# Loading the output rows of one head in eleven small transfers during the attention loop instead of one transfer after the last values

## The chip, the cores and the metric

The kernel runs on one core of a Trainium2 chip. The metric is the device time of one execution in microseconds (us). The figure for the kernel before is the median of 7 runs, 194.99 us, with the runs between 194.86 and 195.08 us. A profile of one execution (its own time is 194.87 us) gives the start and length of every instruction, the packets of the DMA engines, and the time at which each DMA engine reported its part of a transfer as landed.

## What is computed

One decode step: a single token `x` of 512 numbers is normalised; an attention branch of 32 heads reads the last 4096 keys and values of a long cache; a small MLP branch makes a gate; the two are joined.

```python
xn = _layernorm(x)
# attention branch, W = 4096, 32 heads of 128
q = (xn @ wq).reshape(B, Sq, Hq, Dh).transpose(0, 2, 1, 3)
k = k_cache[:, :, Sk - W:, :]
v = v_cache[:, :, Sk - W:, :]
p = softmax(einsum("bhqd,bhkd->bhqk", q, k) * Dh ** -0.5)
o = einsum("bhqk,bhkd->bhqd", p, v)
s = o.transpose(0, 2, 1, 3).reshape(B, Sq, Hq * Dh) @ wo
# gate: an MLP of xn
out = x + s * silu(B(xn))
```

Keys and values are bf16. For 32 heads they are 32 MB and 32 MB, `wq` and `wo` are 4 MB each, and the MLP's weights about 3 MB, so nearly 79 MB are read once and little is done with each byte.

## The kernel before, in words

The 32 heads are worked through in `NG = 8` groups of `G = 4`. A group's keys are one tile `kv` of 128 partitions x 128 columns x 128 numbers (4 MB), and so are its values. The loop at L513 runs `s` from 0 to 9. Step `s` loads and scores the keys of group `s`; the values belong to group `h = s - LAG`, two steps behind. Keys have three buffers (`K_BUFS`), values two (`V_BUFS`).

All large loads are issued by one queue, SyncE's (SP), in the order in which the program names them (`load`, L78). An SP load waits, on the queue, until the buffer that it will fill has been read for the last time and until its semaphore is free: there are eight semaphores for DMAs, used in turn, so a load also waits for the landing of the load eight places before it. The order of the instructions on TensorE (PE), VectorE (DVE) and ScalarE (ACT) is the program's own inside the loop (`manual_schedule`, L509).

The loads before the loop are the MLP's weights `w2`, `w3`, `w4`, two loads of 20 rows each into `w4_few` (L97), and `wq` (L101). The loop's loads on SP are then: keys 0 (in two halves), 1 and 2; values 0; keys 3, values 1; keys 4, values 2; keys 5, values 3, and the rows of `wo` for heads 0 to 15; keys 6, values 4; keys 7, values 5, and the rows of `wo` for heads 16 to 23 and 24 to 27; values 6; values 7. Values 7 come in four pieces of 64, 32, 16 and 16 columns (`cuts`, L508). Behind them come the rows of `wo` for heads 28 to 31, 128 rows of 512 numbers (1 KB) for each head, into the tile `wo_rows` [128 partitions, 4 heads, 512]: heads 28 and 29 in one DMA, 30 in one, 31 in one (L524). This is the last load before the output.

The end of the program (L595 to L609): PE multiplies the pieces of values 7 with the probabilities as they land (`v_part`, L440: 64, then 32 + 16, then 16 matmuls), DVE divides the result (`v_out`, L457), PE adds the four heads' output to the sum `y_ps` with `y_head` (L505; four matmuls for each head against `wo_row(h)`, recorded at L156 because `rows_add` makes them), DVE applies the gate (L606) and adds `x` (L608), and SP stores 1 KB (L609). `y_block(2)` a little earlier does the same kind and number of matmuls (16, L156) for heads 24 to 27.

The memory of `wo_rows` and of the value buffers is taken at step `s = LAG` (L517 to L521), from the place where the weights (`wts`) stood until then.

Of the kernel before, what the change touches and what calls it, by code (L numbers as in the profile page):

```python
# [8 lines left out]
P = 128  # L9
# [9 lines left out]
G = 4  # L19
LAG = 2  # L20
# [9 lines left out]
def kernel(  # L30
# [18 lines left out]
    _, H, Sk, Dh = A_k_cache.shape  # L49
# [28 lines left out]
    def load(dst, src):  # L78
        return tc.keep_in_program_order(nc.sync.dma_start(out=dst, in_=src))
# [23 lines left out]
    def load_kv(pool, cache, g, cuts=(0, CP)):  # L103
        t = pool.tile([P, CP, Dh], BF16, tag="kv", name="kv")
        src = cache[0, G * g:G * g + G, W0:, :].rearrange("a (b c) d -> b a (c d)", b=PB)
        dst = t[:].rearrange("p c d -> p (c d)")
        for c0, c1 in zip(cuts, cuts[1:]):
            load(dst[:, c0 * Dh:c1 * Dh], src[:, :, c0 * Dh:c1 * Dh])
        return t
# [43 lines left out]
    def rows_add(ps, col, w, last):  # L153
        k = col.shape[0]
        for j in range(KC):
            nc.tensor.matmul(ps[32 * j:32 * j + 1, :], lhsT=col, rhs=w[0:k, j * P:(j + 1) * P],  # L156
                             start=False, stop=last, skip_group_check=True)
# [161 lines left out]
    def k_open(g):  # L319
        st[g] = {  # L320
            "sT": ps_s.tile([P, CP - 64, G], FP32, tag="sT", name="sT"),
            "S": sm_pool.tile([P, CP], FP32, tag="S", name="S"),
        }

    def k_vector(g, kn, part):
        m = nd(g) // 4
        rows = slice(m * part, m * part + m)
        prod = prod_pool.tile([P, 20, Dh], BF16, tag="prod", name="prod")
        nc.vector.tensor_tensor(out=prod[:, 0:m, :], in0=kn[:, rows, :],  # L329
                                in1=q_bc[:, g:g + 1, :].to_broadcast([P, m, Dh]), op=ALU.mult)  # L330
        nc.vector.tensor_reduce(out=st[g]["S"][:, rows], in_=prod[:, 0:m, :], axis=AX.X, op=ALU.add)  # L331
# [3 lines left out]
    def batches(g):  # L335
        n, m = nd(g), CP - nd(g)
        k = -(-m // 8)
        edges = [n + m * i // k for i in range(k + 1)]
        return list(zip(edges, edges[1:]))

    def k_turn(g, kn, b):
        c0, c1 = batches(g)[b]
        pt = ps_tr.tile([P, 8, P], BF16, tag="pt", name="pt")
        for c in range(c0, c1):
            nc.tensor.transpose(pt[:, c - c0, :], kn[:, c, :], ident_bf[:])  # L345
        kts[b] = kt_pool.tile([P, 8, P], BF16, tag="kt", name="kt")
        nc.scalar.copy(out=kts[b][:, 0:c1 - c0, :], in_=pt[:, 0:c1 - c0, :])  # L347

    def k_scores(g, b):
        kt = kts.pop(b)  # L350
        c0, c1 = batches(g)[b]
        for c in range(c0, c1):
            nc.tensor.matmul(st[g]["sT"][:, c - nd(g), :], lhsT=kt[:, c - c0, :],  # L353
                             rhs=qT_bf[:, G * g:G * g + G], start=True, stop=True)


    def sm_own(g):
        s = st[g]
        m = CP - nd(g)
        s["own"] = sm_pool.tile([P, CP - 64, G], FP32, tag="own", bufs=1, name="own")  # L360
        for a in range(G):
            nc.scalar.mul(s["own"][:, 0:m, a], s["sT"][:, 0:m, a], par[:, a:a + 1])  # L362
# [31 lines left out]
    def sm_den(g):  # L394
        s = st[g]
        s["den"] = ps_misc.tile([P, G], FP32, tag="misc", name="den_ps")
        nc.tensor.matmul(s["den"][:], lhsT=ones_f[:], rhs=s["sum"][:], start=True, stop=True)

    def sm_rden(g):
        s = st[g]  # L400
        s["rden"] = sm_pool.tile([P, G], FP32, tag="rden", name="rden")
        nc.vector.reciprocal(out=s["rden"][:], in_=s["den"][:])  # L402
# [7 lines left out]
    def load_wo(i):  # L410
        h0, n = blocks[i]
        load(wo_blk[i], A_wo[h0 * P:(h0 + n) * P, :].rearrange("(p t) n -> p t n", p=P))
# [4 lines left out]
    def load_rows(h, n):  # L417
        load(wo_rows[:, h - h_part:h - h_part + n, :],
             A_wo[h * P:(h + n) * P, :].rearrange("(h p) n -> p h n", p=P))
# [23 lines left out]
    def v_add(g):  # L443
        s = st[g]
        s["oT"] = ps_misc.tile([P, G], FP32, tag="misc", name="oT")
        for j in range(4):
            nc.tensor.matmul(s["oT"][:], lhsT=s["ov_sb"][:, j, :], rhs=fold[:, G * j:G * j + G],  # L447
                             start=(j == 0), stop=(j == 3))

    def v_out(g):  # L450
        h = G * g
        b = [i for i, (h0, _) in enumerate(blocks) if h >= h0][-1]
        if b not in o_blk:
            o_blk[b] = sm_pool.tile([P, blocks[b][1]], BF16, tag=f"o{b}", bufs=1, name="o")
        c = h - blocks[b][0]
        if g >= NG - 3:
            nc.vector.tensor_tensor(out=o_blk[b][:, c:c + G], in0=st[g]["oT"][:], in1=st[g]["rden"][:],  # L457
                                    op=ALU.mult)
            return
        for k in range(G):  # L460
            nc.scalar.mul(o_blk[b][:, c + k:c + k + 1], st[g]["oT"][:, k:k + 1], st[g]["rden"][:, k:k + 1])  # L461
# [48 lines left out]
                                         mybir.EngineType.Activation})  # L510
    region.__enter__()
    v_pool = None
    for s in range(NG + LAG):  # L513
        h = s - LAG
        last = h == NG - 1
        kn = load_kv(k_pool, A_k_cache, s, (0, 64, CP) if s == 0 else (0, CP)) if s < NG else None
        if s == LAG:  # L517
            wts_guard.__exit__(None, None, None)
            v_pool = ctx.enter_context(tc.tile_pool(name="v", bufs=V_BUFS))
            wo_blk[2] = v_pool.tile([P, 4, D], BF16, tag="wo_4", bufs=1, name="wo_4")  # L520
            wo_rows = v_pool.tile([P, H - h_part, D], BF16, tag="wo_rows", bufs=1, name="wo_rows")  # L521
        if last:
            v = load_kv(v_pool, A_v_cache, h, cuts)
            for r, n in ((H - G, 2), (H - 2, 1), (H - 1, 1)):  # L524
                load_rows(r, n)
        elif h >= 0:
            v = load_kv(v_pool, A_v_cache, h)
        if h == 3:
            wo_24 = k_pool.tile([P, 32, D], BF16, tag="kv", name="wo_24")
            wo_blk[0], wo_blk[1] = wo_24[:, 0:16, :], wo_24[:, 16:24, :]  # L530
            load_wo(0)
        if h == 5:
            load_wo(1)
            load_wo(2)

        if s < NG:
            nb = len(batches(s))

            def keys(b0, b1):
                for b in range(b0, b1):  # L540
                    k_turn(s, kn, b)
                    if b > 0:
                        k_scores(s, b - 1)

            k_open(s)
            k_vector(s, kn, 0)
            keys(0, 2)
            if s > 1:
                sm_den(s - 2)
                sm_rden(s - 2)  # L550
            if h - 1 in MOVED:
                v_add(h - 1)
                v_out(h - 1)
            if s == 7:
                rows_add(y_ps, one_f, y_row, False)
            keys(2, 4)
            k_vector(s, kn, 1)
            if s > 0:
                sm_turn(s - 1)
            if s == 6:  # L560
                ox_spread(0)
            keys(4, nb)
            k_scores(s, nb - 1)
            sm_own(s)
            if s > 0:
                sm_exp(s - 1)
            k_vector(s, kn, 2)
            if s == 6:
                ox_pick(0)
            k_vector(s, kn, 3)  # L570
            if h >= 0:
                v_part(h, v)
            sm_max(s)
            if s == 6:
                y_wide(0, 0, 16)
            if h >= 0 and h not in MOVED:
                v_out(h)
        elif s == NG:

            sm_den(NG - 2)  # L580
            sm_rden(NG - 2)
            sm_turn(NG - 1)
            sm_exp(NG - 1)
            v_add(h - 1)
            v_out(h - 1)
            ox_spread(1)
            ox_pick(1)
            sm_den(NG - 1)
            sm_rden(NG - 1)
            y_block(1)  # L590
            v_part(h, v)
            v_add(h)
            v_out(h)
            ox_spread(2)
        else:  # L595
            v_part(h, v, 0, cuts[1])
            ox_pick(2)
            y_block(2)
            for c0, c1 in zip(cuts[1:], cuts[2:]):
                v_part(h, v, c0, c1)  # L600
            v_out(h)
            for r in range(H - G, H):
                y_head(r)
# [36 lines left out]
```

## Time and profile before

| | |
|---|---|
| median of 7 runs | 194.99 us (194.86 to 195.08) |
| the profiled execution | 194.87 us, its span 193.1 us |
| PE busy | 138.2 us, 72% of the span |
| DVE busy | 145.6 us, 75% |
| ACT busy | 90.7 us, 47% |
| bytes read from HBM | 78.84 MB, 408 GB/s over the span |
| share of the 16 DMA engines taken by SP's queue (q1) | 96.0% |
| last SP load of values 7 issued | 173.63 us from the start of the span |
| three `wo_rows` loads issued | 174.28 us and the two after it |
| output store issued | 190.35 us |

The span is the time that the profile covers; the 1.8 us that are missing to the execution's own time lie around it. The page gives a share of busy time for each engine and a row for the DMA engines. A share is an average; which wait ends last at a place is read from the chain of waits and from the timeline. "16 DMA engines" are sixteen movers that share each transfer: every one moves its part, and a transfer has landed when all that take part have reported.

### The profile page before, as it was taken

The page shows a single profiled execution, that of the slowest core. Times are in us where ns is not written, and L with a number is a line of the kernel's source. Part 1 is how long each engine was busy: PE and PEld are TensorE (multiplying, and loading weights), DVE is VectorE, ACT ScalarE, POOL GpSimd, SP SyncE. Part 2 cuts the span into 40 slices and gives each one's busy share as a digit, 9 for nine tenths or more (in the row PEclk, how much of TensorE's full clock was granted, in tenths as well). Part 3 has the DMA queues.
Part 4 walks back from the last instruction along what each step waited for, and adds up shares of the span by engine and source line. Part 5 has one row for each costly group of instructions (what it writes and reads, how often), then busy time and mean ns, then how long its engine had stood idle before and what let it go on. Part 6 is the DMA issues. An engine that isn't in the chain of part 4 may idle for free.

```text
span 193.1 us, 3919 instructions
## 1 busy us (share of the span) xinstructions
PE 138.2 (72%) x1696; PEld 99.9 (52%) x1696; DVE 145.6 (75%) x168; ACT 90.7 (47%) x197; POOL 5.9 (3%) x12
## 2 busy tenths in 40 slices
PE   0548978989965169429787892875497989877882
PEld 0437248868854153328547632851395348636371
DVE  1580021999999999998999999999999988962011
ACT  2002001888778354407873753474358245863100
POOL 8210000000000000000000000000000000000000
PEclk9999985555555555855876558587655596695755
DMA  6999999999999999999999998999999999999980
GB/s 211 414 434 434 424 434 441 426 434 431 434 431 436 434 424 434 434 434 434 431 428 434 424 428 384 455 428 434 438 421 428 433 428 389 452 431 411 403 315 5
DMA packets 4722, 79.08 MB, mean 410 GB/s; under 512 B 666, under 2 KB 1210, under 8 KB 1722
## 3 DMA queue, kind: packets, MB, share of 16 engines
q1 hardware_dynamic: 4554, 78.84, 96.0%
q8 instruction: 13, 0.21, 0.5%
q10 hardware_dynamic: 152, 0.00, 0.0%
q14 instruction: 3, 0.02, 0.0%
HBM read 78.84 MB, written 0.00 MB: 408 GB/s over the span
## 4 chain that ended last, share of the span: by engine, by line
DVE 50%; PE 29%; DMA 9%; ACT 4%; issue 4%; SPq 1%; POOL 0%; POOLq 0%; ACTq 0%
DVE S L331 29%; DVE prod L329 15%; DMA kv<-in_A_v_cache_dram 7%; PE pt L345 6%; PE oT L447 4%; ACT kt L347 3%; PE hr_ps L255 3%; PE ov L431 3%; PE a_ps L236 2%; PE sT L353 2%; DMA x_bf<-in_A_x_dram 2%; PE yr_ps L495 2%; PE qT_ps L271 2%; PE hr_ps L250 1%; DVE S L367 1%
## 5 line engine op out<-in xcount | busy, mean ns | idle before, releaser
L331 DVE TENSOR_REDUCE S<-prod 128x20 f32<-128x2560 bf16 (+2 forms) x32 | 82.2, 2570 | 1.1
L347 ACT COPY kt<-pt 128x1024 bf16<-128x1024 bf16 (+1 forms) x56 | 55.2, 1005 | 16.7 <-PE pt L345 15.7
L345 PE MATMUL pt<-ident_bf,kv 128*128 128x128 bf16 x444 | 51.4, 293 | 2.3 <-DMA kv<-in_A_k_cache_dram 2.3
L345 PEld LDWEIGHTS <-kv 128*128 128x128 bf16 x444 | 41.9, 136 | 7.2 <-issue 3.5
L329 DVE TENSOR_TENSOR prod<-kv,q_bc 128x2560 bf16<-128x2560 bf16 (+2 forms) x32 | 43.5, 1359 | 1.6 <-ACT q_bc L285 1.3
L353 PE MATMUL sT<-qT_bf,kt 128*128 128x4 bf16 x444 | 20.9, 169 | 13.2 <-ACT kt L347 12.2
L353 PEld LDWEIGHTS <-kt 128*128 128x128 bf16 x444 | 17.6, 106 | 21.1 <-ACT kt L347 20.6
L431 PE MATMUL ov<-kv,pT 128*16 128x512 bf16 x224 | 22.3, 569 | 0.0
L447 PE MATMUL oT<-fold,ov_sb 128*128 128x4 f32 x56 | 11.5, 328 | 13.8 <-DVE rden L402 12.8
L447 PEld LDWEIGHTS oT<-fold,ov_sb 128*128 128x128 f32 x56 | 10.8, 288 | 14.8 <-DVE rden L402 13.3
L391 ACT ACTIVATE pT<-S,mb 128x128 bf16<-128x128 f32 x32 | 14.0, 578 | 0.3
L461 ACT ACTIVATE o<-oT,rden 128x1 bf16<-128x1 f32 x20 | 3.6, 264 | 20.3 <-PE oT L447 20.3
L431 PEld LDWEIGHTS <-pT 128*16 128x16 bf16 x224 | 6.4, 116 | 12.9 <-issue 11.9
L435 ACT COPY ov_sb<-ov 128x512 f32<-128x512 f32 x7 | 4.1, 589 | 15.3 <-PE ov L431 15.3
L362 ACT ACTIVATE own<-sT,par 128x48 f32<-128x48 f32 (+2 forms) x32 | 7.6, 361 | 3.7 <-PE sT L353 3.7
L457 DVE TENSOR_TENSOR o<-oT,rden 128x4 bf16<-128x4 f32 x3 | 0.5, 163 | 11.2 <-PE oT L447 8.3
L391 ACT ACTIVATION_READ_ACCUMULATOR pT<-S,mb 128x1 f32 x32 | 8.4, 263 | 0.0
L239 ACT ACTIVATE a_bf<-a_ps 128x8 bf16<-128x8 f32 x1 | 0.2, 178 | 14.4 <-PE a_ps L236 14.4
L258 DVE COPY hr<-hr_ps 1x512 f32<-1x512 f32 x1 | 0.7, 679 | 7.5 <-PE hr_ps L255 7.5
L375 PE MATMUL mt_ps<-ident_f,m 128*1 128x128 f32 x8 | 2.9, 360 | 4.4 <-DVE rden L402 4.4
L236 PE MATMUL a_ps<-z_bf,w_sb 128*128 128x1 bf16 (+2 forms) x68 | 4.8, 204 | 1.5 <-DVE z_bf L219 1.5
L236 PEld LDWEIGHTS <-w_sb 128*128 128x128 bf16 (+2 forms) x68 | 5.0, 168 | 1.6 <-issue 1.6
(119 smaller groups left out, 101.8 us busy)
## 6 DMA issues: line engine op xcount, KB each, us to landing
kv<-in_A_k_cache_dram SPq DMA_DIRECT2D x7, 4096.0 KB, 30.8
kv<-in_A_v_cache_dram SPq DMA_DIRECT2D x7, 4096.0 KB, 29.0
wq_sb<-in_A_wq_dram SPq DMA_DIRECT2D x1, 4096.0 KB, 16.3
kv<-in_A_k_cache_dram SPq DMA_DIRECT2D x2, 2048.0 KB, 20.5
wo<-in_A_wo_dram SPq DMA_DIRECT2D x1, 2048.0 KB, 25.6
kv<-in_A_v_cache_dram SPq DMA_DIRECT2D x1, 2048.0 KB, 11.3
w_sb<-in_B_w_dram SPq DMA_DIRECT2D x1, 1376.0 KB
w_sb<-in_B_w_dram SPq DMA_DIRECT2D x1, 1024.0 KB, 8.9
```

The source lines that it names most:

```text
L236: nc.tensor.matmul(a_ps[0:m, j:j + 1], lhsT=w3_cols(c, j), rhs=z3_bf[:, c:c + 1], start=(c == 0), stop=(c == KC - 1))
L255: nc.tensor.matmul(hr_ps[:], lhsT=act, rhs=w, start=False, stop=(i == len(chunks) - 1))
L329: nc.vector.tensor_tensor(out=prod[:, 0:m, :], in0=kn[:, rows, :], in1=q_bc[:, g:g + 1, :].to_broadcast([P, m, Dh]), op=ALU.mult)
L331: nc.vector.tensor_reduce(out=st[g]["S"][:, rows], in_=prod[:, 0:m, :], axis=AX.X, op=ALU.add)
L345: nc.tensor.transpose(pt[:, c - c0, :], kn[:, c, :], ident_bf[:])
L347: nc.scalar.copy(out=kts[b][:, 0:c1 - c0, :], in_=pt[:, 0:c1 - c0, :])
L353: nc.tensor.matmul(st[g]["sT"][:, c - nd(g), :], lhsT=kt[:, c - c0, :], rhs=qT_bf[:, G * g:G * g + G], start=True, stop=True)
L362: nc.scalar.mul(s["own"][:, 0:m, a], s["sT"][:, 0:m, a], par[:, a:a + 1])
L391: nc.scalar.activation(out=s["pT"][:, :, a], in_=s["S"][:], func=ACT.Exp, scale=scale, bias=mb[:, a:a + 1], accum_out=s["sum"][:, a:a + 1])
L431: nc.tensor.matmul(s["ov"][r:r + 4 * G], lhsT=s["pT"][:, c:c + 4, :].rearrange("p i a -> p (i a)"), rhs=v[:, c:c + 4, :], start=False, sto ...
L435: nc.scalar.copy(out=s["ov_sb"][:], in_=s["ov"][:])
L447: nc.tensor.matmul(s["oT"][:], lhsT=s["ov_sb"][:, j, :], rhs=fold[:, G * j:G * j + G], start=(j == 0), stop=(j == 3))
```

## The change

The 128 rows of head 28 are no longer loaded with those of head 29 behind values 7. They are loaded in eleven pieces of 15, 14, 13, 12, 11, 10, 9, 7, 6, 15 and 16 rows, into the same place (`wo_rows[p0:p0 + n, 0, :]`), between step 2 and step 7. The pieces stand in SP's queue: two behind values 0; then one each behind keys 3, values 1, keys 4, values 2, keys 5, values 3, keys 6, values 4, keys 7. Values 5, 6 and 7 have none behind them. Behind values 7 there are still three loads: heads 29, 30 and 31, one DMA of 128 KB each. The number of bytes is the same; SP issues eleven DMAs more. PE, DVE, ACT and POOL have the same instructions in the same order as before.

```diff
     v_pool = None
+    early_rows, p0 = {}, 0
+    for i, n in enumerate((15, 14, 13, 12, 11, 10, 9, 7, 6, 15, 16)):
+        early_rows.setdefault(LAG + i // 2, []).append((p0, n))
+        p0 += n
+    assert p0 == P
     for s in range(NG + LAG):
         h = s - LAG
         last = h == NG - 1
         kn = load_kv(k_pool, A_k_cache, s, (0, 64, CP) if s == 0 else (0, CP)) if s < NG else None
+        if s > LAG:
+            p0, n = early_rows.get(s, [(0, 0)]).pop(0)
+            if n:
+                load(wo_rows[p0:p0 + n, 0, :], A_wo[(H - G) * P + p0:(H - G) * P + p0 + n, :])
         if s == LAG:
             wts_guard.__exit__(None, None, None)
...
         if last:
             v = load_kv(v_pool, A_v_cache, h, cuts)
-            for r, n in ((H - G, 2), (H - 2, 1), (H - 1, 1)):
-                load_rows(r, n)
+            for r in range(H - G + 1, H):
+                load_rows(r, 1)
         elif h >= 0:
             v = load_kv(v_pool, A_v_cache, h)
+        for p0, n in early_rows.get(s, ()):
+            load(wo_rows[p0:p0 + n, 0, :], A_wo[(H - G) * P + p0:(H - G) * P + p0 + n, :])
```

## The prediction

> **What bounds the kernel now.** I read the page's slices first, to see which resource never rests.
>
> ```profile
> DVE  1580021999999999998999999999999988962011
> ...
> DMA  6999999999999999999999998999999999999980
> ...
> q1 hardware_dynamic: 4554, 78.84, 96.0%
> ```
>
> The DMA row stands at 9 from the second slice to the last but two. DVE rests from slice 34 on. So a byte moved earlier doesn't fill a hole: there is none, it pushes what is behind it. What matters is the order on the DMA engines and who waits for what at the end. I read that from the chain of waits in the last 30 us (start, length, what).
>
> ```profile
> 171.76 0.54 SPq L79
> ...
> 173.63 14.37 DMA kv<-in_A_v_cache_dram
> ...
> 188.05 0.60 PE oT L440 x16
> ...
> 188.68 0.17 DVE o L457
> ...
> 188.90 0.79 PE y_ps L156 x15
> ...
> 189.70 0.30 DVE y L606
> ```
>
> The chain runs through the last piece of values 7 (landed 188.01), not through the output rows. Values 7 were issued at 171.76, but values 6 were still arriving (landed 178.12 by the trace's landing records), so those 14 us are queueing behind earlier bytes. Then the tail, in windows (columns after the clock of PE: share of the 16 DMA engines, GB/s):
>
> ```profile
> 186.60:187.00 0.40, 0.40 (x20) 0.40 (x19) 0.00 (x0) 0.00 (x0) 0.00 (x0) 0.50 0.66 246
> ...
> 187.80:188.20 0.40, 0.24 (x9) 0.16 (x7) 0.00 (x0) 0.00 (x0) 0.00 (x0) 0.50 0.40 141
> 188.20:188.50 0.30, 0.30 (x16) 0.30 (x14) 0.00 (x0) 0.00 (x0) 0.00 (x0) 0.50 0.23 79
> 188.50:188.90 0.40, 0.14 (x8) 0.06 (x4) 0.16 (x1) 0.00 (x0) 0.00 (x0) 0.50 0.07 23
> ```
>
> The engines don't finish together. A share of 0.66 is 10.6 engines, 0.40 is 6.4, and 0.07 is one engine alone at 23 GB/s. The landing records say the same: the sixteen reports for the last piece of values 7 run from 184.31 to 188.01, for head 31 from 185.78 to 189.34, the last three at 188.74, 188.98, 189.34. One engine is last with everything, by about 0.35 us.
>
> Which engine? In the records for `wq`, the first large load behind the two `w4_few` loads, eleven engines report at 19.96 to 21.70 and five together at 22.37 to 22.48. Five engines carry both 160 KB loads of 20 rows, 64 KB each, 2.4 us; that was not spread over sixteen. The lead is never given back, since no engine runs dry: values 0 end at 58.87 to 60.48 on eleven engines and 61.31 to 62.27 on five. Later fetches of instructions push other engines back by about 1.5 us each, to within 0.6 us of the last, but the last two in each list stay two of these five, by following the lists load to load.
>
> **The change, part by part.**
>
> *Removed from the tail.* Head 28's rows are 8 packets of 1 KB on each engine. On the last engine heads 30 and 31 are reported 0.325 us apart, so the rows of head 31 come 0.33 us sooner relative to values 7.
>
> *Added ahead of values 7.* All eleven pieces are in front of values 7 in SP's queue. The question is how many rows the last engine gets. Bounds: 0 and 11, one from each piece; evenly spread it would be 8. I take 11: both 20-row loads fell on the same five engines, so a load that can't use all sixteen takes a fixed set, not a rotating one, and I take it that a load on six or more engines includes those five. Then the five slow engines carry 11 KB where they carried 8, and the engines outside a small set carry least.
>
> [...]
>
> *Cost of one row.* Eight packets in 0.325 us are 41 ns each; one engine alone at 23 GB/s gives 1 KB in 44 ns. Between transfers there is a report: the early 32-row load, two packets and a report on each engine, lies 0.091 us behind its predecessor, so 48 ns for one row with its report. A 4 MB load takes 9.71 us per engine against 9.69 for eight packets 1.211 apart, so a boundary between large loads is up to 20 ns. One row then costs 48 to 62 ns; I take the middle, 55. No row shows a lone 1 KB packet among 32 KB ones. Far bounds: 38 ns (1 KB at 27 GB/s, the boundary free), or 0.325 us (as much as a whole 128 KB load), which is 3.6 us for eleven.
>
> *Sum.* Values 7 land 11 x 0.055 = 0.605 us later: 188.61. The 16 matmuls, DVE's division and the start of `y_head` follow with the same gaps: 188.90 becomes 189.50. Then something is given back:
>
> ```profile
> 185.93 0.59 PE L156 MATMUL y_ps<-wo,ox 128*1 128x128 bf16 x16 [0.48 <-DVE ox L482]
> ...
> 188.90 0.76 PE L156 MATMUL y_ps<-wo_rows,o 128*1 128x128 bf16 x16 [0.26 <-DVE o L457]
> 189.38 0.09 PEld L156 LDWEIGHTS <-o 128*1 128x1 bf16 x3 [0.19 <-issue]
> ```
>
> The same 16 matmuls took 0.59 without a late load and 0.76 at the end, where the last weights start at 189.38, just behind head 31's landing at 189.34. After the change heads 29 to 31 land 0.33 apart behind 188.61, head 31 at 189.6, while PE reaches its four matmuls at about 189.5 + 0.44 = 189.9. So that wait of 0.17 goes. Net: 0.605 - 0.17 = +0.43 us.
>
> *What hides the rest.* Eleven SP issues of 0.43 to 0.6 us (the `wo_rows` and K/V issues) cost about 6 us of SP, which is idle between loads: keys 4 at 60.58, values 2 at 77.30. Three loads directly follow a piece: values 1 (46.09) moves to 46.7, the 16-head rows (99.86) to 100.4, values 5 (132.91) to 133.1. Each is issued more than 15 us before its engines are free (values 1 behind keys 3, which the first engine ends at 68.58), so nothing moves; without that lead each would cost its 0.5 us. Pieces also take their turn among eight semaphores. The worst are the piece behind keys 4, which waits for values 0 (landed 62.27) and goes 1.1 us after it could, with values 2 behind it at 77.30; and `wo` for heads 24 to 27, issued at about 134.6 instead of 134.1, which waits for keys 6 (135.17) with values 6 behind it at 153.09. Keys and values reach the slow engines up to 0.6 us later through the loop; waits of PE for keys in the profile are two, both at the start, before any piece. Values 6 would land at 178.72 and be used from 178.76, the first piece of values 7 at 183.63 against 183.61 and its delay is eaten by the wait at 188.05. If values 6 came later than that, ACT and PE up to 183.5 would shift, and the 0.2 us of idle before 188.05 would take most of it.
>
> [...]
>
> In the profiled execution: 194.87 + 0.43 = 195.30, span 193.5. Its own time is 0.12 below the median; against the median the forecast is 194.99 + 0.43 = 195.42.
>
> **The rivals.**
>
> *A. The slow engine is relieved.* If the larger sets don't hold the five (if they sit at the other end), the last engine gets 1 to 4 rows: values 7 land 0.05 to 0.2 later, head 31 about 0.13 to 0.29 earlier. For the likely middle, 2 rows: 188.90 becomes 189.01, plus 0.59 is 189.60 against 189.66, so -0.06; at best, 1 row, -0.12. Time 194.87 to 194.95: not slower. It decides when the last engine gets 3 rows or fewer (3 x 0.055 = 0.165, less than the 0.17 given back). For it: nothing in the profile names engines. Against it: the same five twice.
>
> *B. A lone small packet costs more.* If an engine drains before it goes on, one row costs like a 4 KB packet, 0.158 us (the third piece of values 7 to the fourth: 1.234 us for 8). 11 x 0.158 - 0.17 = +1.57: 196.56. For it: no such mix in the trace. Against: the 32-row load's 0.091 us.
>
> *C. Evenly spread.* If the pieces' engines follow the partition, the last engine carries its 8 rows as before, only earlier: 8 x 0.055 - 0.17 = +0.27, so 195.26. Against it: the 20 rows fell on five engines equally, 4 each.
>
> **How the numbers follow.** Forecast 0.62, A 0.16, B 0.10, C 0.12. A measurement of this kernel tells 0.2% (0.39 us, above 195.38 or below 194.60) from no change. The forecast's own span, 48 to 62 ns, gives 195.35 to 195.50; with some spread of the matmuls' timing 195.25 to 195.65, on the slower side for two thirds: 0.41 slower, 0.21 same. B is slower (0.10), C is same (0.12), A is same but for 0.03 that I leave for faster. Faster 0.03, same 0.46, slower 0.51. The range reaches from A's middle, 194.93, to 195.85, a row at 94 ns.
>
> **What would show it.** Each step has its mark in the changed profile: the last piece of values 7 landing near 188.6; PE's 16 matmuls of L440 starting there; the 16 of `wo_rows` taking 0.6 without the late weights; the sixteen reports of head 31 spread wider, the light engines ending earlier and the five later; PE and DVE before 178 where they were. The prediction is wrong if values 7 land no later than 188.2 (A), or past 189.2 (B), or if a large load is issued late behind a piece and engines go idle before 183.

## The result and the profile after

| | median | runs |
|---|---|---|
| before | 195.08 us | 60, from 194.79 |
| changed | 196.35 us | 23, from 196.04 |

The changed kernel is slower: 1.0065 times before, 95% interval 1.0046 to 1.0085, which is +0.9 to +1.7 us. The forecast was +0.43 and its range ended at 195.85, so the sign was right and the size was not: the loss is about three times as large. The first profile of the changed kernel fell in a disturbed execution (199.23 us); the profile shown here is of the same kernel run again, an execution of 196.75 us with a span of 194.7.

The DMA engines are nearly as full as before. The page's slices and queues:

```profile
DVE  1580012999999999998999999997999996963011
...
DMA  5999999999999999999999999999999999999980
...
q1 hardware_dynamic: 4682, 78.84, 95.7%
```

SP's queue has 128 packets more than before (4682 against 4554: the pieces' reports; rows and bytes are the same) and no idle slice, but everything arrives later. One short gap is hidden in these slices: from 175.5 to 176.0 us the packet records fill 13.6 of the sixteen engines (16.1, which is full, before), since values 7 were issued late. The end of the program, from the timeline (start, length, engine, line, operation; in brackets what ended the idle time):

```profile
185.88 1.77 PE L440 MATMUL oT<-pT,kv 128*128 128x4 bf16 x64
...
188.69 1.86 PE L440 MATMUL oT<-pT,kv 128*128 128x4 bf16 x64
...
190.81 0.59 PE L156 MATMUL y_ps<-wo_rows,o 128*1 128x128 bf16 x16 [0.26 <-DVE o L457]
191.46 0.29 DVE L617 TENSOR_TENSOR y<-y_ps,g_row 128x128 f32<-128x128 f32 x1 [0.70 <-PE y_ps L156]
```

The tail in windows (PE clock, share of the DMA engines, GB/s at the end of each line):

```profile
186.60:187.00 0.40, 0.40 (x22) 0.40 (x20) 0.00 (x0) 0.00 (x0) 0.00 (x0) 1.00 0.94 353
187.80:188.20 0.40, 0.04 (x4) 0.04 (x8) 0.27 (x2) 0.00 (x0) 0.00 (x0) 0.50 0.68 266
188.20:188.50 0.30, 0.30 (x16) 0.27 (x16) 0.00 (x0) 0.00 (x0) 0.00 (x0) 0.50 0.54 198
188.50:188.90 0.40, 0.40 (x20) 0.21 (x9) 0.00 (x0) 0.00 (x0) 0.00 (x0) 0.50 0.58 205
```

Where one engine was left before (0.07 from 188.50 on) nine are still at work (0.58). That not a few slow engines are late, but all, is clearer in the landing records: the sixteen reports for values 6, set in order against the sixteen of before, are 1.2 to 1.9 us late, the first and the last 1.41. For the last piece of values 7 the three earliest reports are 2.3 to 2.8 us late, which is the gap above; the last one, which the program waits for, is 1.43 late and owes nothing to that gap.

The 16 matmuls of `y_head` take 0.59 us, without the late weights of before (0.76): that part of the forecast holds. But the last piece of values 7 landed at 189.44, 1.43 us later than before (188.01), not 0.6. And PE is late by itself: its first 64 matmuls of values 7 start at 185.88 instead of 183.61 (the line of before is below), so the other 64 run in one block up to 190.55. Had just 16 of them been left after the landing at 189.44, they would have ended near 190.1: in this execution the late PE costs about 0.5 us on top of the late landing, and 0.17 is given back.

```profile
183.61 1.80 PE L440 MATMUL oT<-pT,kv 128*128 128x4 bf16 x64
```

DVE, in the middle of the loop, shows where the lateness of PE begins:

```profile
134.74 0.28 DVE L369 TENSOR_REDUCE m<-S 128x1 f32<-128x128 f32 x1
136.22 1.49 DVE L329 TENSOR_TENSOR prod<-kv,q_bc 128x2560 bf16<-128x2560 bf16 x1 [1.20 <-DMA kv<-in_A_k_cache_dram]
...
156.27 1.22 DVE L329 TENSOR_TENSOR prod<-kv,q_bc 128x2048 bf16<-128x2048 bf16 x1 [0.23 <-DMA kv<-in_A_k_cache_dram]
```

Keys 6 landed at 136.19 and keys 7 at 156.25, and DVE stood waiting for both. Before, they landed at 135.17 and 154.95 and DVE began the same work at 135.31 and 155.05 without a wait:

```profile
135.31 1.48 DVE L329 TENSOR_TENSOR prod<-kv,q_bc 128x2560 bf16<-128x2560 bf16 x1
...
155.05 1.22 DVE L329 TENSOR_TENSOR prod<-kv,q_bc 128x2048 bf16<-128x2048 bf16 x1
```

The chain of waits of the changed kernel has changed its course accordingly:

```profile
131.65 24.60 DMA kv<-in_A_k_cache_dram
...
156.27 1.24 DVE prod L329
...
170.04 0.36 PE sT L353 x8
...
171.46 2.88 PE ov L431 x23
```

and of the kernel before in the same place:

```profile
168.90 0.35 PE sT L353 x8
...
169.88 1.86 PE ov L431 x32
```

Keys 7 now hold the chain for 24.6 us, then DVE, PE and the reuse of a value buffer lead from there to the issue of values 7 (174.39; before 171.76). Of these 2.6 us, 1.14 are there at `sT` (170.04 against 168.90), carried on from DVE's late start on keys 7 (1.22). The other 1.5 come from PE, whose matmuls of values 5 (`ov`; the chain shows a part of them) took 2.95 us by the timeline instead of 1.90: its granted clock was 0.64 from 171.4 to 174.4, where it was 1.00 from 169.5 to 172.0 before. Two chains, the queue's and the computation's, are late by more than the sum allowed, and both start in the DMA queue during the loop; the low clock of PE comes on top in the second.

### The profile page after: what moved, and what is told of

The parts are those of the page before. It is cut to its first block, busy times and chain, and to the rows that moved or that the text cites. A ratio compares the mean times of both kernels' runs of the same rounds, so it can differ in the third digit from the quotient of the medians.

```text
span 197.2 us, 3930 instructions
## 1 busy us (share of the span) xinstructions
PE 136.1 (69%) x1696; PEld 97.5 (49%) x1696; DVE 145.5 (74%) x168; ACT 90.0 (46%) x197; POOL 5.9 (3%) x12
## 3 DMA queue, kind: packets, MB, share of 16 engines
q1 hardware_dynamic: 4682, 78.84, 94.7%
## 4 chain that ended last, share of the span: by engine, by line
DVE 38%; PE 36%; DMA 14%; ACT 6%; issue 4%; POOL 0%; POOLq 0%; ACTq 0%
DVE S L331 22%; DMA kv<-in_A_k_cache_dram 12%; DVE prod L329 11%; PE ov L431 6%; PE oT L447 5%; PE pt L345 5%; ACT kt L347 4%; PE hr_ps L255 3%; PE a_ps L236 2%; PE yr_ps L495 2%; DMA x_bf<-in_A_x_dram 2%; PE sT L353 2%; PE oT L440 2%; PE qT_ps L271 2%; PE y_ps L156 1%
## 5 line engine op out<-in xcount | busy, mean ns | idle before, releaser
L347 ACT COPY kt<-pt 128x1024 bf16<-128x1024 bf16 (+1 forms) x56 | 54.6, 1005 | 17.0 <-PE pt L345 16.2
L345 PE MATMUL pt<-ident_bf,kv 128*128 128x128 bf16 x444 | 46.8, 275 | 4.8 <-DMA kv<-in_A_k_cache_dram 4.8
L345 PEld LDWEIGHTS <-kv 128*128 128x128 bf16 x444 | 38.2, 127 | 8.4 <-DMA kv<-in_A_k_cache_dram 6.0
L353 PE MATMUL sT<-qT_bf,kt 128*128 128x4 bf16 x444 | 20.7, 168 | 14.6 <-ACT kt L347 13.6
L447 PE MATMUL oT<-fold,ov_sb 128*128 128x4 f32 x56 | 12.3, 342 | 15.9 <-DVE rden L402 15.0
L447 PEld LDWEIGHTS oT<-fold,ov_sb 128*128 128x128 f32 x56 | 11.7, 308 | 17.4 <-DVE rden L402 15.4
L384 PE MATMUL mb_ps<-md,par_t 5*128 5x4 f32 x16 | 4.2, 332 | 3.8 <-DVE md L379 3.8
```

What stands on the lines that cost most here:

```text
L384: nc.tensor.matmul(mb_ps[:], lhsT=par_t[:].rearrange("k b a -> k (b a)"), rhs=md[:], start=True, stop=True)
```

## The experiments

Times are medians; the kernel before ran on the same chip beside each of them (195.2 us, and 195.75 beside the last experiment, which is not in the table). A difference of 0.3 us is at the edge of what these runs tell apart, so each reading rests on the trace as well. Two quantities are read from the trace's packet records and landing reports for all kernels. The first is the mean length of the 32 KB packets from 33 us on, without those stretched past 1.5 us beside a fetch of instructions (twelve in the kernel before, 1.59 to 1.84 us), and what they take over 1216 ns each, summed and divided by sixteen engines. The second is the first and the last of the sixteen reports for values 6, and the last report of values 7.

```
                        median  ratio to before (95%)      32 KB   over 1216,  values 6        values 7
                        us                                 ns      us/engine   first    last   last
before                  195.2                              1216.7  0.08        174.37  178.12  188.01
the change again        197.07  1.0088 (1.0057-1.0118)     1224.9  0.96        175.78  179.53  189.44
one whole load          195.58  1.0023 (0.9986-1.0059)     1217.2  0.13        174.77  178.75  188.61
eight of 16 rows        196.66  1.0074 (1.0047-1.0100)     1225.9  1.07        175.94  179.51  189.39
into a spare tile       196.41  1.0062 (1.0031-1.0093)     1223.0  0.76        175.74  179.66  189.58
8 rows, every fourth    196.12  1.0026 (0.9997-1.0056)     1216.7  0.08        174.52  179.27  189.21
8 rows, other half      197.63  1.0094 (1.0060-1.0128)     1224.8  0.96        175.49  180.19  190.10
8 rows, adjacent        196.79  1.0053 (1.0023-1.0083)     1219.3  0.36        174.57  179.62  189.62
the same, 256 bytes     195.58  0.9999 (0.9968-1.0029)     1217.6  0.18        174.51  178.85  188.74
```

**The change again, and whether packets slow down.**

> The changed kernel once more, for a profile in an undisturbed run. All theories: about 196.2 us (before 195.0), the last piece of values 7 landing at 189.2 to 189.4 where the kernel before has 188.0. Theory WAKE (each small piece costs its own 0.05 us on the engines that carry it, and also makes the 32 KB packets that follow slower on all sixteen engines for a packet or two): 32 KB packets in the stretches with pieces average 1235 to 1270 ns against 1216 before. Theory SERIAL (a piece costs about 0.11 us on the engines that carry it, nothing elsewhere): 32 KB packets stay at 1216 ns and the engines with few pieces are not late.

The first pieces pass the engines between 58.4 and 62.8 us. In the packets that start from 58 to 62 us the 32 KB ones average 1243 ns, the longest 1295; before, 1216 and 1224. Over the loop 14% of them are longer than 1230 ns, before 0.2%. The first of the sixteen reports for values 6 is 1.41 us late, as late as the last one (1.41). The reports don't name their engines; but the pieces' own rows number one to eleven per engine, 0.05 to 0.55 us, and all sixteen reports are at least 1.2 late, so engines with few pieces are late as well. That is WAKE and not SERIAL. The median, 197.07, is above the 196.2 expected.

**One load in place of eleven.** The rows of head 28 go ahead of values 7 as in the change, but in one load of 128 partitions behind keys 3. Against the changed kernel, abridged:

```diff
-    early_rows, p0 = {}, 0
...
+        if s == 3:
+            load_rows(H - G, 1)
...
-        for p0, n in early_rows.get(s, ()):
-            load(wo_rows[p0:p0 + n, 0, :], A_wo[(H - G) * P + p0:(H - G) * P + p0 + n, :])
```

> The 128 rows of head 28 as one 128-partition load behind keys 3, in place of the eleven pieces. WAKE: the wake comes from the small pieces' form, so only 8 packets of 42 ns go ahead of values 7 and the wait of 0.17 us at the end is given back: +0.17 us, 195.2. SERIAL (0.11 us a row): 8 x 0.11 - 0.17 = +0.7, 195.7. A third, ORDER (it is the bytes put ahead of values 7 that cost, in whatever form): as the changed kernel, 196.0 to 196.2.

195.58, and no wake (1217.2 ns). The chain of waits keeps the course of before, 0.6 us later:

```profile
173.62 14.99 DMA kv<-in_A_v_cache_dram
...
188.66 0.60 PE oT L440 x16
```

ORDER falls: the same bytes ahead of values 7 make them 0.60 late instead of 1.43. The time alone (its interval reaches from 0.9986 to 1.0059) would leave SERIAL's 195.7 standing. The landings don't: values 1 and 2 were 0.42 and 0.43 late against before, near the 0.34 of eight packets and not the 0.88 of SERIAL. Another 0.2 appeared at keys 7, as it did in three of the later kernels, and its cause stays open.

**Eight pieces of 16 rows, evenly on all engines.**

```diff
-    for i, n in enumerate((15, 14, 13, 12, 11, 10, 9, 7, 6, 15, 16)):
+    for i, n in enumerate((16, 16, 16, 16, 16, 16, 16, 16)):
...
-            p0, n = early_rows.get(s, [(0, 0)]).pop(0)
+            p0, n = (early_rows.get(s) or [(0, 0)]).pop(0)
```

> Eight pieces of 16 rows (all sixteen engines, one row each) in the first eight of the places, so the slow engines carry 8 rows instead of 11. WAKE, if the wake goes with rows: 8 x 0.05 + 0.7 - 0.17 = +0.93, 195.95; if it goes with the number of pieces: 8 x 0.05 + 0.5 - 0.17 = +0.73, 195.75. SERIAL: 8 x 0.11 - 0.17 = +0.7, 195.7. If fewer than sixteen engines in a transfer is what disturbs: 8 x 0.05 - 0.17 = +0.23, 195.2.

196.66, above every sum expected (195.2 to 195.95). Neither the eleven rows on the slow five nor the engines that are left out explain the loss: with 8 rows on every engine and all sixteen in each piece, values 7 land within 0.05 of the change's and the packets are as long. The wake did not fall with the number of pieces (1.07 for 8 pieces, 0.96 for 11, both of 128 rows). And the lateness adds up: 8 x 0.05 of their own and 1.07 - 0.08 of wake make 1.39; values 7 landed 1.38 late.

**The pieces into a spare tile, the end left as it was.**

```diff
+            spare = v_pool.tile([P, D], BF16, tag="spare", bufs=1, name="spare")
...
-            for r in range(H - G + 1, H):
-                load_rows(r, 1)
+            for r, n in ((H - G, 2), (H - 2, 1), (H - 1, 1)):
+                load_rows(r, n)
...
-            load(wo_rows[p0:p0 + n, 0, :], A_wo[(H - G) * P + p0:(H - G) * P + p0 + n, :])
+            load(spare[p0:p0 + n, :], A_wo[(H - G) * P + p0:(H - G) * P + p0 + n, :])
```

(The other place where a piece is loaded has the same edit.)

> The eleven pieces go into a spare tile that nobody reads, and the rows of heads 28 and 29 stay behind values 7 as before: the early cost without the relief at the end. The relief is 0.17 us by my sum: 196.2 + 0.17 = 196.4. If the relief is worth the whole 0.33 us of the removed rows: 196.55. If it is worth nothing: 196.2.

196.41, not slower than the change again on the same chip (197.07); the two intervals overlap. Its chain ends in the landing of values 7:

```profile
174.70 14.88 DMA kv<-in_A_v_cache_dram
...
189.63 0.60 PE oT L440 x16
...
190.47 0.75 PE y_ps L156 x12
```

With the four heads behind values 7 again, `y_head` takes 0.75 us again: the 0.16 of relief is in the trace, but no time that these runs can show comes of it. The early pieces alone carry the loss.

**Where the rows are written.** Sixteen extra pieces of 8 rows, two behind each of the first eight loads, from the same source rows in the three kernels, into a spare tile; the end is as before. The kernels differ in the destination's partitions alone. Against the kernel before, without the line that makes the spare tile:

```diff
+    places = iter(range(8))
+
+    def pieces():
+        i = next(places, None)
+        if i is None:
+            return
+        for c in range(2):
+            load(spare[32 * (i // 4) + i % 4:32 * (i // 4) + i % 4 + 29:4, c, :], A_wo[(H - G) * P + 8 * i:(H - G) * P + 8 * i + 8, :])
...
+        if s > LAG:
+            pieces()
...
+            pieces()
```

> The tail as in the kernel before; in the loop sixteen extra pieces of 8 rows (two behind each of the first eight loads) into a spare tile that nobody reads, each piece into every fourth partition of one block of 32 in the lower half. Eight engines carry 16 rows: 16 x 0.05 = 0.8 us of their own on the slow five, in every theory. [...] Theory FORM (any small transfer in the stream leaves a wake, wherever it writes): wake 0.7 to 1.0 us more per engine, 32 KB packets 1224 ns, time 196.6.

For the other half the destination is `spare[64 + 32 * (i // 4) + ...]`, for the adjacent ones `spare[8 * i:8 * i + 8, c, :]`.

> [...] FORM: 196.6, as the other two.

> The same sixteen pieces from the same source rows into eight adjacent partitions each. [...] FORM: 196.6.

196.12, 197.63 and 196.79. FORM falls, and the destination decides. With every fourth partition of the lower half the packets are those of the kernel before (1216.7 ns, 0.08): sixteen small transfers and 128 rows, and no wake. Moved to the upper half, the same transfers leave 0.96 us per engine, and the intervals of the two times (0.9997 to 1.0056 and 1.0060 to 1.0128) don't meet. The adjacent rows, in the lower half again, leave 0.36, about a third of that.

The sixteen reports for keys 6, set in order against those of the spaced kernel, say which engines pay. With the rows in the other half every one is 0.75 to 0.97 us later, so none of the sixteen is spared, though a piece of eight rows, one 1 KB packet each, occupies eight engines at most. With adjacent rows in the lower half the nine earliest stay within 0.21 of the spaced kernel and the other seven are 0.34 to 0.60 later. Which engine writes which partitions is in no record of these runs: they show that the place counts, and neither by what path nor why adjacent rows cost less than rows in the other half. The wait of DVE for keys 6, from its timelines in the spaced and in the other-half kernel, follows the wake:

```profile
135.98 1.49 DVE L329 TENSOR_TENSOR prod<-kv,q_bc 128x2560 bf16<-128x2560 bf16 x1 [0.59 <-DMA kv<-in_A_k_cache_dram]
```

```profile
136.86 1.49 DVE L329 TENSOR_TENSOR prod<-kv,q_bc 128x2560 bf16<-128x2560 bf16 x1 [2.49 <-DMA kv<-in_A_k_cache_dram]
```

(changed: 136.22, shown above; before: 135.31, no wait). With the rows in every fourth partition of the lower half keys 6 land 0.79 us late and DVE starts at 135.98; with the rows in the other half it starts at 136.86. Values 7 land 1.20 late in the spaced kernel, where the rows' own cost was put at 0.8; part of the rest is the 0.2 at keys 7.

**Fewer bytes.** The adjacent pieces with 256 bytes of each row, against the kernel with adjacent rows.

```diff
-            load(spare[8 * i:8 * i + 8, c, :], A_wo[(H - G) * P + 8 * i:(H - G) * P + 8 * i + 8, :])
+            load(spare[8 * i:8 * i + 8, c, 0:128], A_wo[(H - G) * P + 8 * i:(H - G) * P + 8 * i + 8, 0:128])
```

> As the adjacent pieces, but 256 bytes of each row instead of 1 KB. If the wake goes with bytes it falls to a quarter, 0.2 us per engine, and the pieces' own cost to 16 x 0.025 = 0.4 us: 195.6. If it goes with the number of rows or of transfers, it stays at 0.7 to 1.0 us: 196.2 to 196.4.

195.58, and 0.18 us per engine against 0.36. Over the 0.08 that the kernel before has too, 0.10 against 0.28: bytes count, if not quite in proportion (a quarter would be 0.07).

**An attempt to beat both.** Since five engines carry the 20-row loads (five reports for each, at 11.42 to 11.53 us and at 12.65 to 12.77), one of those was split to spread it. Against the kernel before, the new loads alone (the tile that selects the rows was changed to match):

```diff
+            for r0, r1 in ((0, 16), (16, 20)):
+                load(w4_few[32 + r0:32 + r1].rearrange("p t n -> p (t n)"),
+                     B_w4[f0 + 8 * r0:f0 + 8 * r1, :].rearrange("(p t) n -> p (t n)", t=8))
```

> The kernel before, with one of its two 20-row loads of w4_few split into 16 + 4 rows (rows in plain order, the selection tile to match), so that five engines carry 32 KB less and all carry 8 KB more (four of them another 8). If the last engine is one of those five, as the reports say, it ends 0.6 us earlier in its own work (or 0.9 if it is the one without a row of the four) and the next engines 0.3 later: the last piece of values 7 lands 0.2 to 0.35 us sooner, 187.65 to 187.8, time 194.7 to 194.8. If the last engine were another one, it would land 0.3 later, 188.3, time 195.3.

197.69 us, 1.0109 times before (1.0062 to 1.0157): a miss, on the wrong side. The 16-row load puts 8 KB from each of sixteen engines into sixteen adjacent partitions. The windows of this kernel while it runs (last columns: share of the DMA engines, GB/s):

```profile
10.00:12.00 2.00, 0.59 (x2) 0.55 (x3) 1.80 (x12) 0.00 (x0) 0.00 (x0) 1.00 0.91 185
12.00:14.00 2.00, 0.86 (x15) 0.86 (x15) 1.72 (x11) 0.00 (x0) 0.55 (x1) 1.00 1.10 303
```

and of the kernel before in the same stretches:

```profile
10.00:12.00 2.00, 0.59 (x2) 0.55 (x3) 1.80 (x12) 0.00 (x0) 0.00 (x0) 1.00 0.80 337
12.00:14.00 2.00, 0.87 (x15) 0.87 (x15) 1.72 (x11) 0.00 (x0) 0.55 (x1) 1.00 1.22 524
```

The engines are busy and move half as much. That load's reports run from 11.45 to 14.45 us, and `wq` lands at 24.68 instead of 22.48. So the loss arises here: `wq` is 2.2 us late, values 7 still 2.0, and the time is 1.9 longer. I take it for the same effect with large rows; since the number of engines changed with the destination, this kernel doesn't show it by itself. The evenly spread version is no gain as it stands. In the kernel before, the 20 rows are ordered in five groups of four adjacent partitions, and five engines carry four rows each.

## Why the prediction was wrong, by its steps

- *What bounds the kernel, and that bytes moved ahead push what is behind them:* held. The DMA row shows no idle slice. The sign of being wrong that named engines idle before 183 did appear (three of them, near 175.5, behind the late issue of values 7), but not on the engine that is last. The pieces took their turn among the semaphores as described: the `wo` rows for heads 24 to 27 were issued at 136.2, behind the landing of keys 6, with nothing waiting for them until long after.
- *Eleven rows on the slow engines:* held. In the changed kernel the 6-row piece reports about 0.2 us behind each of the five late reports of keys 6 (135.18, 135.28, 135.36, 135.77 and 136.19 by 0.19 to 0.22), so those five are in the smallest set.
- *Cost of one row, 55 ns:* right for the row itself and wrong for what it does. In the packet records two pieces in a row on one engine take 0.10 us, 49 ns each. In the kernel with every fourth partition fourteen of the sixteen rows stood ahead of keys 6, which were 0.79 us late, where values 0, ahead of all rows, were already 0.12 late: 0.67 / 14 is 48 ns. The step that failed is the one behind it, that a row costs only the engine that carries it, so that "the light engines" end earlier. They ended as late as the others: the reports for values 6 span 3.75 us before and after. The sum put the effect on the large packets at nothing; they grew by 0.96 us per engine against 0.08, and the kernels with spaced rows show that this hangs on the partitions into which the rows go. Own cost 11 x 0.05 = 0.55 and wake 0.88 make 1.43; values 7 landed 1.43 late.
- *Rival B* had nearly the right size of loss per row (0.158 us, or 0.154 by its own row, 1.234 / 8; measured 1.43 / 11 = 0.13) and the right time (196.56 against 196.35), by luck: its cause is not there. Two pieces in a row cost 49 ns each, and the extra time is in the large packets of all engines.
- *The 0.17 us given back:* seen (0.59 instead of 0.76), and lost again, since PE was late for another reason.
- *What hides the rest:* failed too. It named the waits of PE and not how close DVE ran behind the keys: 135.31 against 135.17, and 155.05 against 154.95. That cover was 0.1 us thick, and 0.6 us of lateness were already in the sum. With it the computation becomes a second late chain: DVE waits 1.20 and 0.23 us, values 7 are issued 2.6 us later, and PE does 64 matmuls at the end where it did 16. Of the 2.6, 1.1 came through the wait and 1.5 from PE at a clock of 0.64; in the kernel with the spare tile, whose matmuls of values 5 took 1.86 us as before, values 7 were issued 1.06 later, and in the other kernels with pieces 1.2 to 2.8.
- *The tail on one engine:* its lead of 0.35 us at the very end is real, but with all engines late it decided nothing.

## What to carry to other kernels

In these runs the small transfers in the middle of saturated loads weren't priced by their own packets alone: the partitions that they wrote decided. The 8-row pieces in every fourth partition of the lower half left 0.08 us per engine on the large packets, as in the kernel before, the same pieces in the upper half 0.96, and one load of all 128 partitions 0.13. For the same bytes the one whole load made values 7 land 0.60 us later, the eleven pieces 1.43. When a DMA queue is full, a delay in it has to be held against every consumer's start, not only against those that show a wait today; DVE had 0.1 us.

## What was not expected of the hardware

Small transfers slowed the large packets by where they were written. The 128 rows of 1 KB in the eleven pieces lengthened the large packets by 0.88 us in sum per engine, and all sixteen reports for values 6 were 1.2 to 1.9 us late; 128 rows in every fourth partition of the lower half lengthened them by nothing (1216.7 ns, 0.08 us per engine, as before). Sixteen engines writing into sixteen adjacent partitions moved 185 GB/s from 10 to 12 us, where 337 went before, while their busy share stood at 0.91. The runs show the effect, not its path. And a fetch of instructions (16 KB; the page's queue q8 has thirteen) takes one DMA engine about 1.5 us, where 16 KB of a load take 0.6: its packet takes about 1.07 us (0.96 to 1.24 in the kernel before), and the 32 KB packet behind it about 1.7 (1.59 to 1.84) instead of 1.2. The engines don't draw level again: in the kernel before the reports for values 0 are spread over 3.40 us and those for values 6 over 3.75. I take these delays, with the 2.4 us of the five engines that carry the 20-row loads, for the 3.7 us over which the reports for the last piece of values 7 are spread in the kernel before.
